# High and low parts of every stationary operand alternate in memory, 8 bytes apart

## The chip, the core and the metric

The kernel runs on one core of one Trainium2 chip. The metric is the device time of one execution in microseconds (us). Times are the median of repeated runs. A profiled execution gives the views that are read here: busy time of each engine, groups of instructions, waits, the chain of work that ended last, and timelines.

## The reference

The kernel computes a transformer block on `x` of 2048 rows and 640 columns, in float32. Cut to what matters:

```python
mod = (silu(c) @ w_mod).reshape(1, 6, 1, 640)        # sa, ca, ga, sb, cb, gb
h = layernorm(x) * (1 + ca) + sa
q, k, v = split_heads(h @ wqkv)                      # 32 heads of 20
pq, pk = q @ w_phi[head], k @ w_phi[head]
phi = concat([softmax(p), softmax(-p)])              # for q and for k
kv, z = phi_k.T @ v, phi_k.sum(rows)
o = (phi_q @ kv) / (phi_q @ z + 1e-6)
x = x + ga * (o @ wo)
h = layernorm(x) * (1 + cb) + sb
r = relu(h @ w1 + b1) ** 2                           # 640 -> 1728
out = x + gb * (r @ w2 + b2)                         # 1728 -> 640
```

## The kernel before, in words

TensorE multiplies a stationary operand (up to 128x128, put in place by a weight load) with a moving operand that streams through. All large products are made in float32r. To keep float32 accuracy, each operand is held as two parts: a high part (the value rounded to float32r) and a low part (what is left over). A product is then three matmuls that add up in PSUM: high by high, high by low, low by high. `three` writes that list and `mm` (the helper whose line is L81 in the profile) issues it. Since every matmul has its own weight load, the high part of a stationary operand is loaded twice and the low part once for each product.

ACT writes the high part (a copy that rounds), and VectorE (DVE) writes the low part (`lo`, the helper whose line is L91: the full value minus the high part). High and low parts of an operand lie in one tile, but in separate runs: 128 or 256 high values one behind the other, and the low values 1 to 2.5 KB further on. A weight load so reads 128 neighbouring values per partition, 512 bytes.

The rows are worked in 16 tiles of 128 rows, in pairs (`j`, 256 rows). There are four stages:

1. The set-up (0 to about 20 us): `fold` multiplies the projection weights with `w_phi`.
2. The projections (to about 250 us). For each pair, the normalised rows are turned (`t1`, `t_out`) into `HT[j]`, a tile made by `ht` with the axes chunk, part, row. `proj` multiplies it, as the stationary operand, with the folded weights `wk`, `wq` and with `wv` as the moving operand. Each projection tile has two halves: 15 matmuls with 384 moving columns (380 for v) and 15 with 256 (260 for v). In the profile these are `pk`, `pq` and `pv`.
3. The attention output (about 250 to 380 us). `num` makes the numerators in PSUM; `num_hi` and `num_lo` write their parts into `OT[j]`, again a tile of `ht`. For the first two pairs (`DIRECT`) the low part is not made by DVE: a matmul with minus the identity (`neg`, L975) subtracts the high part in PSUM, with the high part as its moving operand. `do_wo` multiplies `OT[j]`, stationary, with `wo`: `pwo`, again 384 and 256 columns.
4. The feed-forward part (about 380 us to the end). `up` has the weights `W1[f]` stationary (tiles `w`) and the turned rows `H2[j]` (tiles `h`, from `ht`) moving: 256 columns. Its output is squared, and for the later pairs recombined (`sums`) for a product scheme with fewer block products. `split_a` and `split_s` write the parts of the squared values and of their sums into tiles `ra` and `rs`. These are stationary in `prod`, with `w2` (tiles `w` and `ring`) moving: `acc` with 384 columns, `acc3x`, `accx` and some of `acc` with 256.

The order of the instructions on each engine is written out by hand in most of the kernel (`manual_schedule`), and a scheduler places the rest. `H2`, `wk`, `wq`, `wv`, `wo` and `w2` are moving operands; `HT`, `OT`, `W1`, `RA` and `RS` are stationary. The last block of `W1` (f = 13) has only 64 columns, and its high and low parts together fill one 128-column load; it is made by the same function.

Of the kernel before, what the change touches and what calls it, by code (L numbers as in the profile page):

```python
# [8 lines left out]
F32 = mybir.dt.float32  # L9
F32R = mybir.dt.float32r  # L10
# [5 lines left out]
P = 128  # L16
# [6 lines left out]
NC = D // P  # L23
# [31 lines left out]
def kernel(  # L55
# [23 lines left out]
    def mm(o, terms, first=True, last=True, skip=False):  # L79
        for i, (a, b) in enumerate(terms):  # L80
            nc.tensor.matmul(  # L81
                o, a, b,
                start=first and i == 0, stop=last and i == len(terms) - 1,
                skip_group_check=skip,
            )
# [4 lines left out]
    def lo(out_lo, full, hi, eng=None):  # L90
        (eng or nc.vector).tensor_tensor(out_lo, full, hi.bitcast(F32), op=ALU.subtract)  # L91
# [18 lines left out]
    def tok2(tag, name, at=0, pool=None):  # L110

        bufs = 1
        if tag == "w":
            tag = f"w{next(w_at)}"
        elif pool is None:
            bufs = BUFS.get(tag, 1)
        t = (pool or mem).tile([P, 2 * D + (W2_AT if tag == 'late' else 128 if tag in W_LONG else 0)], F32, tag=tag, name=name, bufs=bufs)
        return t[:, at : at + 2 * D].rearrange("p (s d) -> p s d", s=2)

    def row(tag, name):  # L120
        return (pc if tag in ("s3", "s4") else mem).tile([P, D], F32, tag=tag, name=name, bufs=BUFS[tag])
# [4 lines left out]
    def wslot(name, tag="w", pool=None):  # L126
        return tok2(tag, name, W2_AT if name.startswith("w2_") else 0, pool).bitcast(F32R)

    def ht(name, j, at=(32, 0)):

        t = mem.tile([P, NC * 512 + (32, 96)[j % 2]], F32R, tag=f"h{j % 2}", name=name, bufs=1)
        at = at[j % 2]
        return t[:, at : at + NC * 512].rearrange("p (d s n) -> p d s n", d=NC, s=2)

    def small(shape, tag, name, bufs=2):
        return (pc if tag in ("mx", "sk", "dn", "dd") else tiny).tile(shape, F32, tag=tag, name=name, bufs=bufs)
# [4 lines left out]
    def tp(name):  # L141
        return psA.tile([P, 512], F32, tag="tp", name=name)
# [152 lines left out]
    def mod_turn(part, p, *cs_):  # L295
        t = MT.setdefault(part, None) or row("s1", f"mt{part}")
        MT[part] = t
        a, n = cs_[0] * P, len(cs_) * P
        for i, c in enumerate(cs_):
            src = by_turn(MA[part])[:, c] if part in (3, 4) else MA[part][:, c * P : (c + 1) * P]  # L300
            nc.tensor.transpose(p[:, i * P : (i + 1) * P], src, ident)
        nc.scalar.activation(t[:, a : a + n], p[:, :n], AF.Copy)

    def mod_sum(part, dest):
        with tc.issue_after(newest(ET_.DVE)):
            nc.vector.tensor_reduce(dest, MT[part].rearrange("p (a b) -> p a b", b=P), axis=AX.X, op=ALU.add)
# [47 lines left out]
    def t_in(xn, d, p, mixed=False):  # L354
        for i in range(2):
            src = by_turn(xn[:, i])[:, d] if mixed else xn[:, i, d * P : (d + 1) * P]
            nc.tensor.transpose(p[:, i * P : (i + 1) * P], src, ident)  # L357
# [7 lines left out]
    def t_out(cols, hT, d, nm, p, hf=None):  # L365
        if hf is None:
            hf = row("s3", f"hf{nm}_{d}")[:, :256]
        nc.scalar.activation(hf, p[:, :256], AF.Identity, bias=cols[:, d : d + 1], scale=cols[:, 5 + d : 6 + d])
        nc.scalar.activation(hT[:, d, 0], hf, AF.Copy)  # L369
        lo(hT[:, d, 1], hf, hT[:, d, 0])  # L370


    HT, PK, EK, EQ, PQ = {}, {}, {}, {}, {}
# [3 lines left out]
    def newest(engine):  # L377
        return next(i for i in reversed(nc.cur_bb.bb.instructions) if i.engine == engine)
# [2 lines left out]

    def t1(j, *ds, more=None):
        if 0 in ds:
            HT[j] = ht(f"hT{j}", j)
        p = tp(f"ta{j}_{ds[0]}")
        for k, d in enumerate(ds):
            t_in(XB[j], d, p[:, 256 * k : 256 * k + 256])
        if more:
            mod_turn(more[0], p[:, 256:], 4)
        for k, d in enumerate(ds):  # L390
            t_out(cols_a, HT[j], d, f"a{j}", p[:, 256 * k : 256 * k + 256])
        DONE[:] = newest(ET_.Activation), newest(ET_.DVE)
        if more:
            mod_sum(*more)

    def proj(nm, t, *between, cut=CUT):
        p = pj(f"p{nm}{t}")
        j, i = divmod(t, 2)
        s = slice(i * P, (i + 1) * P)
        for h, (a, b) in enumerate(cut):  # L400
            terms = []
            for d in range(NC):
                w = W[nm, d]
                terms += three(HT[j][:, d, 0, s], HT[j][:, d, 1, s], w[:, 0, a:b], w[:, 1, a:b])
            done = 0
            for k, at, hook in between:
                if k == h:
                    mm(p[h][:, : b - a], terms[done:at], first=(done == 0), last=False)
                    hook()
                    done = at  # L410
            mm(p[h][:, : b - a], terms[done:], first=(done == 0))
        return p
# [183 lines left out]

    TR = [half(0, 0), half(1, 0), half(1, 1), half(2, 0), half(2, 1)]
    mem.tile([P, 48], F32, tag="gap", name="gap", bufs=1)
    HT[0], HT[1] = ht("hT0", 0), ht("hT1", 1)
    mem.tile([P, 80], F32, tag="gap2", name="gap2", bufs=1)  # L600
    PP = [pj(f"pk{t}") for t in range(0)]

# [101 lines left out]
    for t in range(2, NT - 2):  # L704
        j, i = divmod(t, 2)
# [4 lines left out]
        if t == NT - 4:  # L710
            t1(j + 1, 0, 1)
# [6 lines left out]
        p = proj("v", t, *([(1, 0, lambda: t1(j + 1, 4))] if t == NT - 3 else []), cut=V_CUT)  # L718
# [74 lines left out]
    def bank(nm):  # L793
        return psB.tile([P, 512], F32, tag="m", name=nm)
# [56 lines left out]
    ET, EU, EPT, OT = {}, {}, {}, {}  # L851
# [92 lines left out]
            nc.scalar.activation(t[:124], p[:124].rearrange("p (s n) -> p s n", s=2), AF.Copy)  # L944

    def num(j):
        OT[j] = ht(f"ot{j}", j)
        ps = [bank(f"numa{j}"), bank(f"numb{j}"), tp(f"numc{j}")]
        for g in range(5):
            for c in range(2):  # L950
                mm(ps[g // 2][64 * c : 64 * c + 64, (g % 2) * 256 : (g % 2) * 256 + 256],
                   [(kvd[:, g, 64 * c : 64 * c + 64], EPT[j, g][:124, c])], first=(g % 2 == 0), last=False, skip=True)
        NUM[j] = ps
# [57 lines left out]
    def prep_load(k, f, w):  # L1011
        n = FS[f]
        W = W1 if k == "1" else W2
        if k == "1":
            w = w.rearrange("p s (k n) -> p s k n", k=NC)
        W[f] = w
        i = preps.index((k, f))
        if EARLY_ROWS <= i < EARLY_ROWS + 4:
            if i % 2 == EARLY_ROWS % 2:
                RAWT.append(tok2(f"w{W_AT[(-19, -16)[len(RAWT)]]}", f"rawt{i}"))  # L1020
            raw = RAWT[-1][:, (i - EARLY_ROWS) % 2]
        else:
            raw = row("s1", f"rw{k}_{f}")
        if k == "1":
            raw = raw.rearrange("p (k n) -> p k n", k=NC)
        if k == "1":
            nc.sync.dma_start(raw, w1[f * P : (f + 1) * P].rearrange("p (k n) -> p k n", k=NC))
        else:
            for r in range(P // n):
                nc.sync.dma_start(raw[r * n : r * n + n], w2[f * P : f * P + n])  # L1030
        RAW[k, f] = raw
# [176 lines left out]
    for j in range(NB):  # L1208
        nxt = j + 1 < NB
        b, c = 2 * j + 5, 2 * j + 6  # L1210
# [53 lines left out]
        if nxt:  # L1264
            num(j + 1)
            num_hi(j + 1)
# [7 lines left out]
        if j == 7:  # L1274
            t2(0, 4)
            p = tp("gbt")[:NC, :P]
# [32 lines left out]
    p3 = ctx.enter_context(tc.tile_pool(name="p3", bufs=1, reuse_waits="tile"))  # L1309
# [4 lines left out]
    FT, RA, RS = {}, {}, {}  # L1314
# [31 lines left out]
    def plain(j, n):  # L1346
        return j < PLAIN or n == NF // 2 - 1 or j == NB - 1 and n >= NF // 2 - LAST
# [7 lines left out]
    def split_a(j, n, parts=(0, 1)):  # L1355
        t = FT[j, n]
        if 0 in parts:
            tag = "rs" if j < PLAIN and (NP * j + n) % 2 or (j, n) == (NB - 1, NP - 1) else "ra"
            RA[j, n] = p3.tile([P, 2, 4, P], F32, tag=tag, name=f"ra{j}_{n}").bitcast(F32R)
        a = RA[j, n]  # L1360
        if n < NP - 1:
            nc.scalar.activation(a[:, 0, :3], t[:, :3], AF.Copy)  # L1362
            lo(a[:, 1, :3], t[:, :3], a[:, 0, :3])
        elif 0 in parts:
            nc.scalar.activation(a[:, 0, 0], t[:, A11], AF.Copy)
            lo(a[:, 1, 0], t[:, A11], a[:, 0, 0])
        if plain(j, n) and 0 in parts:
            nc.scalar.activation(a[:, 0, 3], t[:, A21], AF.Copy)
            lo(a[:, 1, 3], t[:, A21], a[:, 0, 3])
        if n == NP - 1 and 1 in parts:  # L1370
            m = FS[-1]
            nc.scalar.activation(a[:m, 0, 1:3], t[:m, 1:3], AF.Copy)
            lo(a[m:, 0, 1:3], t[:m, 1:3], a[:m, 0, 1:3])

    def split_s(j, n):
        t = FT[j, n]
        a = RS[j, n] = p3.tile([P, 2, 4, P], F32, tag="rs", name=f"rs{j}_{n}").bitcast(F32R)
        nc.scalar.activation(a[:, 0], t[:, S1 : S4 + 1], AF.Copy)
        lo(a[:, 1], t[:, S1 : S4 + 1], a[:, 0])

# [408 lines left out]
```

## Time and profile before

| what | value |
|---|---|
| time, median of 3 runs | 747.2 us (746.77 to 747.63) |
| time of the profiled execution | 746.64 us |
| its span, first to last instruction | 744.9 us |
| PE busy | 738.1 us (99%), 6523 matmuls |
| weight loads (PEld) busy | 720.6 us (97%), 6523 loads |
| DVE busy | 598.8 us (80%) |
| ACT busy | 453.1 us (61%) |
| granted TensorE clock | 1.000 |

PE is the matmul side of TensorE, and PEld its weight loads, which overlap the matmul before. The recorded end of a matmul or a load is modelled and they are pipelined: a matmul recorded at 276 ns can be followed by the next one 113 ns later. What a matmul takes of the time is therefore read from the distance of starts: from a row of the chain or the timeline that merges many of them, its length is divided by their count. Differences between two recorded means of the same kind of matmul can be read directly.

### The profile page before, as it was taken

How to read it: one execution, taken by the hardware profiler on the slowest of the kernel's cores; microseconds unless marked ns; L12 is line 12 of the kernel's file. 1: busy time of each engine (PE TensorE's matmuls, PEld its weight loads, DVE VectorE, ACT ScalarE, POOL GpSimd, SP SyncE). 2: the span in 40 equal slices, each digit the busy share in tenths (PEclk: the TensorE clock that was granted, in tenths of full speed). 3: DMA queues.
4: the chain of work that ended last, by engine and by line, in shares of the span. 5: the costliest groups of instructions: out<-in, count | busy, mean ns of one | idle time of the engine just before them, and what ended most of it. 6: DMA issues, size and time to landing. Idle time of an engine off the chain costs nothing.

```text
span 744.9 us, 16612 instructions
## 1 busy us (share of the span) xinstructions
PE 738.1 (99%) x6523; PEld 720.6 (97%) x6523; DVE 598.8 (80%) x1089; ACT 453.1 (61%) x1028; POOL 169.1 (23%) x352
## 2 busy tenths in 40 slices
PE   9999999999999999999999999999999999999997
PEld 9999999999999988998999999999999999999997
DVE  6598988987999999999755777877786776777766
ACT  5767566657863355567687667475574747647431
POOL 2000101001100337547303040231321313222110
PEclk9999999999999999999999999999999999999999
DMA  8812341343331254754885567897667768667461
GB/s 330 339 37 106 111 134 59 107 143 107 126 124 72 83 184 152 173 137 106 209 251 166 154 199 255 271 312 211 180 190 201 214 184 240 187 176 213 129 183 36
DMA packets 58800, 126.46 MB, mean 170 GB/s; under 512 B 7438, under 2 KB 16403, under 8 KB 58723
## 3 DMA queue, kind: packets, MB, share of 16 engines
q1 hardware_dynamic: 38636, 79.20, 32.4%
q0 software_dynamic: 17504, 40.90, 22.1%
q10 hardware_dynamic: 2583, 5.30, 1.9%
q8 instruction: 51, 0.84, 0.5%
q14 instruction: 26, 0.21, 0.1%
HBM read 100.74 MB, written 29.89 MB: 175 GB/s over the span
## 4 chain that ended last, share of the span: by engine, by line
PE 88%; DVE 6%; ACT 3%; POOL 1%; issue 1%; ACTq 0%; DVEq 0%; POOLq 0%
PE up L81 25%; PE acc L81 18%; PE pk L81 8%; PE pwo L81 8%; PE pv L81 8%; PE pq L81 6%; PE acc3x L81 5%; PE te L943 2%; PE kvp L448 1%; DVE dn L875 1%; PE foldk L275 1%; PE numa L81 1%; PE ta L357 1%; DVE scr L873 1%; PE foldq L275 1%
## 5 line engine op out<-in xcount | busy, mean ns | idle before, releaser
L81 PE MATMUL up<-h,w 128*128 128x256 f32 x1640 | 204.6, 276 | 0.1
L81 PEld LDWEIGHTS up<-h,w 128*128 128x128 f32 x1640 | 196.5, 188 | 0.7 <-DVE h L91 0.5
L1338 ACT ACTIVATE ft<-up,b_t 128x256 f32<-128x256 f32 x104 | 49.2, 473 | 95.6 <-PE up L81 95.2
L81 PE MATMUL acc<-w,ra 128*128 128x384 f32 x452 | 97.5, 335 | 0.0
L1339 DVE TENSOR_TENSOR ft<-ft 128x256 f32<-128x256 f32 x104 | 43.8, 421 | 43.0 <-ACT ft L1338 41.5
L81 PE MATMUL pwo<-wo,ot 128*128 128x384 f32 (+1 forms) x480 | 78.1, 313 | 0.0
L81 PE MATMUL pq<-wq,hT 128*128 128x384 f32 (+1 forms) x480 | 75.8, 312 | 0.0
L81 PEld LDWEIGHTS acc<-w,ra 128*128 128x128 f32 x452 | 72.7, 188 | 0.8 <-DVE ra L91 0.6
L81 PE MATMUL pk<-wk,hT 128*128 128x384 f32 (+1 forms) x480 | 73.1, 309 | 0.0
L81 PE MATMUL pv<-wv,hT 128*128 128x380 f32 (+1 forms) x480 | 73.0, 309 | 0.0
L81 PEld LDWEIGHTS pwo<-wo,ot 128*128 128x128 f32 x480 | 69.5, 188 | 2.8 <-issue 2.7
L81 PEld LDWEIGHTS pq<-wq,hT 128*128 128x128 f32 x480 | 71.3, 188 | 0.7 <-issue 0.5
L81 PEld LDWEIGHTS pv<-wv,hT 128*128 128x128 f32 x480 | 71.3, 188 | 0.0
L81 PEld LDWEIGHTS pk<-wk,hT 128*128 128x128 f32 x480 | 70.8, 188 | 0.5 <-ACT hT L369 0.2
L91 DVE TENSOR_TENSOR ra<-ft,ra 128x384 fp32r<-128x384 f32 (+2 forms) x86 | 36.8, 448 | 32.6 <-ACT ra L1362 18.8
L1448 POOL DMA_DIRECT2D ring_a<-td_a x34 | 18.5, 543 | 117.2 <-PE acc L81 103.5
L1362 ACT ACTIVATE ra<-ft 128x384 fp32r<-128x384 f32 x48 | 25.2, 526 | 28.4 <-DVE ft L1339 22.3
L81 PE MATMUL acc3x<-w,ra 128*128 128x256 f32 x231 | 39.5, 278 | 0.0
L81 PEld LDWEIGHTS acc3x<-w,ra 128*128 128x128 f32 x231 | 37.2, 188 | 0.0
L439 DVE TENSOR_REDUCE sk<-ek 128x64 f32<-128x1280 f32 x16 | 23.7, 1482 | 15.1 <-ACT ek L434 10.7
L1353 DVE TENSOR_TENSOR ft<-ft 128x128 f32<-128x128 f32 x136 | 33.3, 286 | 1.2
L334 POOL TENSOR_SCALAR sma<-sma 128x2 f32<-128x2 f32 x6 | 3.1, 516 | 134.9 <-ACT xb L333 134.9
(255 smaller groups left out, 1442.5 us busy)
## 6 DMA issues: line engine op xcount, KB each, us to landing
ring_c<-td_c POOLq DMA_DIRECT2D x34, 384.0 KB, 4.0
ring_a<-td_a POOLq DMA_DIRECT2D x34, 384.0 KB, 3.4
ring_b<-td_b POOLq DMA_DIRECT2D x34, 256.0 KB, 3.6
esp<-eq SPq DMA_DIRECT2D x12, 640.0 KB
el<-esp SPq DMA_DIRECT2D x12, 640.0 KB
rw<-in_w SPq DMA_DIRECT2D x23, 320.0 KB
wm<-in_w_mod SPq DMA_DIRECT2D x20, 320.0 KB
xb<-in_x SPq DMA_DIRECT2D x8, 640.0 KB
```

The source lines that it names most:

```text
L81: nc.tensor.matmul(o, a, b, start=first and i == 0, stop=last and i == len(terms) - 1, skip_group_check=skip,)
L91: (eng or nc.vector).tensor_tensor(out_lo, full, hi.bitcast(F32), op=ALU.subtract)
L275: nc.tensor.matmul(p[g // 3][:, (g % 3) * 120 : (g % 3) * 120 + n], r, bd_t[:120, g * 120 : g * 120 + n], start=True, stop=True,)
L357: nc.tensor.transpose(p[:, i * P : (i + 1) * P], src, ident)
L439: nc.vector.tensor_reduce(s, heads(flat(e)), axis=AX.X, op=ALU.add)
L448: nc.tensor.matmul(kvp[0][32 * c : 32 * c + DH + 1, a - g % 3 * DH : a - g % 3 * DH + 2 * m].rearrange("p (s n) -> p s n", s=2)[:, :, h % ...
L943: nc.tensor.transpose(p[:124, a : a + P], EU[2 * j + i][:, 2 * g + c, :124], ident)
L1338: nc.scalar.activation(r, p, AF.Relu, bias=b1_t[:, f : f + 1])
L1339: nc.vector.tensor_tensor(r, r, r, op=ALU.mult)
L1353: nc.vector.tensor_tensor(t[:, o], t[:, a], t[:, b], op=op)
L1362: nc.scalar.activation(a[:, 0, :3], t[:, :3], AF.Copy)
L1448: nc.gpsimd.dma_start(RING[j, n, r], TD[n][r].bitcast(F32R))
```

## The change

Every stationary operand that has two parts changes its order in memory. The axes of its tile are now chunk, column, part, where they were chunk, part, column (or part, chunk, column): high and low values alternate, so neighbouring values of one part are 8 bytes apart, and the low value lies 4 bytes behind its high value. Sizes and places of the tiles stay the same. The edit is made by a new flag of `ht` and by views:

```diff
-    def ht(name, j, at=(32, 0)):
+    def ht(name, j, at=(32, 0), mixed=False):
...
-        return t[:, at : at + NC * 512].rearrange("p (d s n) -> p d s n", d=NC, s=2)
+        t = t[:, at : at + NC * 512]
+        return t.rearrange("p (d n s) -> p d s n", d=NC, s=2) if mixed else t.rearrange("p (d s n) -> p d s n", d=NC, s=2)
...
-            HT[j] = ht(f"hT{j}", j)
+            HT[j] = ht(f"hT{j}", j, mixed=True)
...
-    HT[0], HT[1] = ht("hT0", 0), ht("hT1", 1)
+    HT[0], HT[1] = ht("hT0", 0, mixed=True), ht("hT1", 1, mixed=True)
...
-        OT[j] = ht(f"ot{j}", j)
+        OT[j] = ht(f"ot{j}", j, mixed=True)
...
-            w = w.rearrange("p s (k n) -> p s k n", k=NC)
+            w = w.rearrange("p s d -> p (s d)").rearrange("p (k n s) -> p s k n", k=NC, s=2) if n == P else w.rearrange("p s (k n) -> p s k n", k=NC)
...
-            RA[j, n] = p3.tile([P, 2, 4, P], F32, tag=tag, name=f"ra{j}_{n}").bitcast(F32R)
+            RA[j, n] = p3.tile([P, 2, 4, P], F32, tag=tag, name=f"ra{j}_{n}").rearrange("p a b n -> p (a b n)").rearrange("p (b n s) -> p s b n", b=4, s=2).bitcast(F32R)
...
-        a = RS[j, n] = p3.tile([P, 2, 4, P], F32, tag="rs", name=f"rs{j}_{n}").bitcast(F32R)
+        a = RS[j, n] = p3.tile([P, 2, 4, P], F32, tag="rs", name=f"rs{j}_{n}").rearrange("p a b n -> p (a b n)").rearrange("p (b n s) -> p s b n", b=4, s=2).bitcast(F32R)
```

`H2` and the temporary rows that also come from `ht` keep the old order, and so does the 64-column block of `W1`. The order of the instructions on every engine, their count and what each waits for stay as they were; ACT's and DVE's writes of the parts, DVE's reads of the high part and TensorE's loads step by 8 bytes where they stepped by 4. The six matmuls with `neg` read the high part of `OT` as their moving operand, so these too step by 8 bytes. DMAs touch none of these tiles.

## The prediction

> **What bounds the kernel now.** I read the page first: how busy each engine is.
>
> ```profile
> PE 738.1 (99%) x6523; PEld 720.6 (97%) x6523; DVE 598.8 (80%) x1089; ACT 453.1 (61%) x1028; POOL 169.1 (23%) x352
> ```
>
> PE is busy for all but 7 us of the 744.9 us span, so waiting is not the matter. Next the busy times by stage: projections, attention output, and four stretches of the feed-forward part (columns: length, then PE, PEld, DVE, ACT, POOL, granted clock, DMA share, GB/s).
>
> ```profile
> 60.00:250.00 190.00, 188.98 (x2241) 185.87 (x2240) 170.47 (x218) 120.37 (x258) 17.86 (x27) 1.00 0.32 105
> 278.00:370.00 92.00, 91.41 (x688) 82.09 (x687) 83.28 (x101) 56.51 (x128) 54.00 (x97) 1.00 0.60 152
> 384.00:480.00 96.00, 96.00 (x755) 95.56 (x754) 71.06 (x157) 63.64 (x148) 17.56 (x48) 1.00 0.67 212
> 480.00:560.00 80.00, 80.00 (x631) 80.00 (x630) 61.49 (x157) 52.66 (x127) 22.34 (x43) 1.00 0.81 230
> ```
>
> From 384 us on PE never stands still, and in the two stages before it stands still for 1.6 us of 282. The granted clock is 1.00 throughout. The time is therefore the sum of the distances at which matmuls follow each other. This change touches nothing but how the stationary operands are laid out, so I need those distances. The chain of work gives them (start, length, count): each row is an unbroken run of matmuls.
>
> ```profile
> 81.02 4.40 PE pk L81 x30
> 125.91 4.43 PE pk L81 x30
> 139.90 4.30 PE pk L81 x30
> 732.06 2.83 PE up L81 x25
> 735.58 2.08 PE acc L81 x12
> ```
>
> A 256-column matmul takes 2.83/25 = 0.113 us, a 384-column one 2.08/12 = 0.173. The three `pk` rows are the same 30 matmuls (15 of each width) on three row tiles, and yet differ by up to 0.13 us. 15 x (0.173 + 0.113) is 4.29, the best of them. So there is a small loss of up to 3% that comes and goes with something that is not the work itself. The recorded means, by shape, show where it sits:
>
> ```profile
> L81 PE MATMUL up<-h,w 128*128 128x256 f32 x1640 | 204.6, 276 | 0.1
> L81 PE MATMUL acc<-w,ra 128*128 128x384 f32 x452 | 97.5, 335 | 0.0
> L81 PE MATMUL pwo<-wo,ot 128*128 128x384 f32 x240 | 47.3, 342 | 0.0
> L81 PE MATMUL pk<-wk,hT 128*128 128x384 f32 x240 | 46.7, 340 | 0.0
> L81 PE MATMUL pq<-wq,hT 128*128 128x384 f32 x240 | 46.1, 342 | 0.0
> L81 PE MATMUL pv<-wv,hT 128*128 128x380 f32 x240 | 44.3, 336 | 0.0
> L81 PE MATMUL acc3x<-w,ra 128*128 128x256 f32 x231 | 39.5, 278 | 0.0
> L81 PE MATMUL pwo<-wo,ot 128*128 128x256 f32 x240 | 32.9, 285 | 0.0
> L81 PE MATMUL pq<-wq,hT 128*128 128x256 f32 x240 | 32.3, 282 | 0.0
> L81 PE MATMUL pk<-wk,hT 128*128 128x256 f32 x240 | 31.6, 278 | 0.0
> L81 PE MATMUL acc<-ring_a,rs 128*128 128x384 f32 x102 | 23.1, 334 | 0.0
> L81 PE MATMUL acc<-w,rs 128*128 128x256 f32 x102 | 17.2, 277 | 0.0
> L81 PE MATMUL acc<-ring_b,rs 128*128 128x256 f32 x102 | 17.1, 276 | 0.0
> L81 PE MATMUL acc3x<-w,rs 128*128 128x256 f32 x102 | 17.1, 276 | 0.0
> ```
>
> The least means are 276 for 256 columns and 334 for 384. The feed-forward part is close to them; the projections and `pwo` lie 2 to 9 ns above.
>
> **The change part by part.** Order, count and waits of all instructions stay, so no instruction moves and no wait is added or removed. Five prices are left.
>
> First, the distance of matmuls in an undisturbed run. Does the load that runs beside a matmul slow the stream? The matmuls with `neg` answer, since two of them have no load beside them and two do (PE and PEld, start and length).
>
> ```profile
> 267.28 0.50 PE L975 MATMUL numb<-ot,neg 128*128 128x512 f32 x1
> 267.27 0.19 PEld L975 LDWEIGHTS numb<-ot,neg 128*128 128x128 f32 x1
> 267.55 0.19 PEld L975 LDWEIGHTS numc<-ot,neg 128*128 128x128 f32 x1
> 267.61 0.33 PE L975 MATMUL numc<-ot,neg 128*128 128x256 f32 x1
> 282.00 0.40 PE L975 MATMUL numb<-ot,neg 128*128 128x512 f32 x1
> 282.23 0.28 PE L975 MATMUL numc<-ot,neg 128*128 128x256 f32 x1
> 282.00 0.19 PEld L975 LDWEIGHTS numc<-ot,neg 128*128 128x128 f32 x1
> ```
>
> At 282.00 the next load starts with the matmul, and the next matmul follows after 0.23 us. At 267.28 the matmul first has to wait for its own load, and the next load comes only at the end: recorded 0.50 against 0.40, so 0.10 for the exposed load and again 0.23 for the stream. The stream runs at 0.44 to 0.45 ns a column with or without a load beside it. The change to the load's reading pattern can therefore not be expected to free the stream itself: price 0 for that, with the end below nothing in the second rival.
>
> Second, the losses above the least means. Over these: pk 6 x 240, pq and pwo 8 x 240 each, pv 2 x 240, acc 1 x 452 (384 or 380 columns: 6.2 us); pk 2, pq 6 and pwo 9 x 240, acc3x 2 x 231 (256 columns: 4.5 us); in all 10.7 us. Part of it is not the stream's: in `pq` and `pwo` other work is put between matmuls, and the first matmul after it carries a load that nothing hides, which the change leaves alone. The rest depends on how load and stream lie to each other, as the `pk` rows show: same addresses from tile to tile, other lengths. A contiguous load moves through 64 bytes while the stream moves through 128 (128 columns against 256 in the same 0.113 us), so they drift against each other. With a step of 8 bytes a load covers 1 KB in the time in which a 256-column stream covers 1 KB: they keep step. I take half of the 10.7 us as the gain, 5 us; ends 0 and 10.7.
>
> Third, the load itself. It must take less than 0.113 us or it becomes the bound of the 256-column matmuls. What a load needs when it reads one value behind the other, and when it steps, is shown by turning matmuls (128 columns, little to stream):
>
> ```profile
> 262.00 1.15 PE L943 MATMUL te<-ident,ezb 128*124 128x128 f32 x9
> 120.10 0.65 PE L301 MATMUL mc<-ident,wm 128*128 128x128 f32 x4
> 151.91 0.73 PE L301 MATMUL mc<-ident,wm 128*128 128x128 f32 x4
> ```
>
> Nine `te` in 1.15 us, less the last one's length of about 0.27, are 0.11 us each with loads of neighbouring values. Of the two `mc` rows the first loads neighbouring values and the second steps by 20 bytes (`by_turn`): 0.08 us more for four, 20 ns a load. So a step of 20 bytes costs up to 20 ns. For a step of 8 bytes the ends are 0 and 20 ns on top of 0.11 us; the first 3 ns are hidden under the 0.113. I take 0, being the end that is nearer to 8 bytes if the cost comes from reaching too few values in one piece of memory; the third rival takes the other way.
> [...]
>
> Fourth, the writes. DVE's `lo` now reads and writes with a step of 8 bytes, ACT writes with it. The only row with DVE reading at a step (20 bytes) is the transposing one:
>
> ```profile
> L1128 DVE STREAM_TRANSPOSE xm<-xx 128x640 f32<-128x640 f32 x16 | 21.8, 1362 | 2.7 <-ACT xx L1165 2.7
> L91 DVE TENSOR_TENSOR w<-rw,w 128x640 fp32r<-128x640 f32 x22 | 17.5, 826 | 2.8 <-ACT w L1037 2.5
> L91 DVE TENSOR_TENSOR ot<-numa,ot 128x512 fp32r<-128x512 f32 x6 | 4.1, 683 | 1.5 <-ACT ot L966 1.5
> ```
>
> 1362 against 826 for 640 elements is 1.65 times, and it is another operation: the far end. In the feed-forward part DVE has 18 of 80 us to spare, so even that stays beside the matmuls. In the attention stage it has 8.7 of 92 us; three `ot` operations a pair (two of 0.68, one of 0.41) at 1.65 times are 1.2 us for each of six pairs, 7 us, of which nearly all fits. I take 0; ends 0 and +5.
>
> Fifth, the six `neg` matmuls stream the high part with the new step: 4 x 0.23 + 2 x 0.12 = 1.2 us in all, taken at 0, doubled at worst: +1.2.
>
> The sum against the profiled execution: 746.6 - 5 = 741.6. Its span is 744.9 and 1.7 lie around it; the median of the runs shown is 0.6 above it, so 742.
>
> **The rivals.** Nothing changes: the loads are hidden before and after, and the lengths of the runs stay as mixed as they are. For it speaks the `neg` reading: a load beside a stream costs the stream nothing. Against it speak the unequal `pk` rows. It gives 747.
> [...]
>
> Freed further: if the stream's 0.113 us came from the two reading side by side after all, the 256-column matmuls could fall to the 0.11 of a load. These are 1560 of `up` (the 80 of its last block keep their layout), 231 + 720 of `acc3x`, `pk`, `pq`, `pwo` and 306 on `rs`: 2817, times 3 ns is 8.5 us, and with the whole 10.7 us 19: 728. The `neg` rows speak against it.
>
> Slower: the load becomes the bound. If a load with 8-byte steps takes 0.118 us, 8 ns more, 5 ns of that show in each of the 2817 matmuls: 14 us, 761. It decides from 3 ns on; the 384-column ones hide it with 60 ns to spare. For it: the load must touch twice as much memory, a step of 20 bytes costs up to 20 ns, and only 3 ns are free. Against it: 8 bytes is a much smaller step. At 4 ns more it is 1 ns a matmul, 750; at the far end of 20 ns it is 48 us.
>
> That the change doesn't do what it says is no rival: all five kinds of stationary operands take the new step.
>
> **How the numbers follow.** Forecast (in step) 0.34, freed further 0.10, nothing 0.22, load as bound 0.34. A run tells 0.2%, 1.5 us, from no change. Forecast and freed further are faster but for a few per cent; of nothing, most stays within 1.5 us, and its rest goes both ways, as the mixture of run lengths may shift by a us or two: faster 0.43, same 0.20, slower 0.37. Both signs hold much, so the forecast's own range stands here: 736 to 747, the ends of its gain. The whole range has to reach the freed case at 728 with 2 us for noise and order, and 762 for the load at 8 ns; beyond lie a dearer load and a freer stream, together 2 in 10.
>
> **What would show it.** Right: `up` rows stay at 276 or lower, the 384-column means of `pk`, `pq` and `pwo` come down to 334 to 336 and the 256-column ones to 276 to 278, and all `pk` runs of 30 take the same 4.3 us or less. The load as bound: all 256-column means rise by the same few ns, `up` included, while the 384-column ones stay. DVE at fault: the L91 rows of `ra`, `rs`, `ot`, `hT` grow, and PEld waits for them. Freed: `up` falls below 0.113 us a matmul. The prediction is wrong if the means of `up` or `acc` change by more than 2 ns, for it leaves the undisturbed stream as it is.

## The result, and the profile after

The changed kernel takes 765.5 us (median of 4 runs, 765.17 to 766.0) against 747.0 before: a ratio of 1.0247, interval 1.0229 to 1.0265. It is 18.5 us slower where 742 was forecast, and 3.5 us beyond the upper end of the range. Of the rivals, "the load becomes the bound", priced at 761, is nearest.

First the busy times of the page, and the first and the last of the four stretches by stage (columns as before: length, then PE, PEld, DVE, ACT, POOL, granted clock, DMA share, GB/s).

```profile
PE 759.3 (99%) x6523; PEld 743.1 (97%) x6523; DVE 601.1 (79%) x1089; ACT 458.7 (60%) x1028; POOL 167.0 (22%) x352
```

```profile
60.00:250.00 190.00, 190.00 (x2244) 187.96 (x2242) 170.69 (x217) 121.58 (x256) 15.28 (x27) 1.00 0.32 105
480.00:560.00 80.00, 80.00 (x601) 80.00 (x600) 58.42 (x149) 47.80 (x114) 21.67 (x41) 1.00 0.81 232
```

PE stands still no more than before and the clock is still 1.00, but fewer matmuls fit into the same stretch: 601 instead of 631 in the last one. So it is the distances again. The chain of work of the changed kernel (start, length, count):

```profile
141.97 4.46 PE pk L81 x30
157.84 4.47 PE pk L81 x30
747.52 1.80 PE up L81 x15
751.09 2.94 PE up L81 x25
754.75 2.12 PE acc L81 x12
```

Fifteen `up` take 1.80 us, 0.120 us each, where it was 0.113. The run of 25 holds its own control: its last ten belong to the block of `W1` that kept its order, and 2.94 - 1.80 leaves 0.114 us for each of these. A 384-column `acc` takes 2.12/12 = 0.177 instead of 0.173. The `pk` runs of 30 are now all alike, as the forecast said, but at 4.46 and not at 4.3: 15 x (0.120 + 0.177) is 4.46.

The recorded means by shape of the changed kernel show that all of these groups moved:

```profile
L81 PE MATMUL up<-h,w 128*128 128x256 f32 x1640 | 214.9, 282 | 0.1
L81 PE MATMUL acc<-w,ra 128*128 128x384 f32 x452 | 98.8, 339 | 0.0
L81 PE MATMUL pk<-wk,hT 128*128 128x384 f32 x240 | 47.2, 342 | 0.0
L81 PE MATMUL acc3x<-w,ra 128*128 128x256 f32 x231 | 40.5, 282 | 0.0
L81 PE MATMUL pwo<-wo,ot 128*128 128x256 f32 x240 | 34.2, 290 | 0.0
L81 PE MATMUL pk<-wk,hT 128*128 128x256 f32 x240 | 32.7, 282 | 0.0
L81 PE MATMUL acc<-ring_b,rs 128*128 128x256 f32 x102 | 17.8, 283 | 0.0
L449 PE MATMUL kvp<-ek,vt 128*21 128x40 f32 x1024 | 11.9, 203 | 0.0
```

Added up over all groups of this view (busy time and the idle time just before it, after less before): `up` 10.3 us, the other 256-column groups 6.5, those of 384 and 380 columns 4.1, `neg` 1.0, the rest -2.3. That is 19.6, and the span grew by 19.4, from 744.9 to 764.3. The rest is mostly `kvp`, with 1.1 us less of busy and 0.9 us less of idle time; why was not looked into. Its row before, and two rows of the loads before:

```profile
L448 PE MATMUL kvp<-ek,vt 128*21 128x40 f32 x1024 | 13.0, 203 | 0.9 <-issue 0.9
L81 PEld LDWEIGHTS up<-h,w 128*128 128x128 f32 x1640 | 196.5, 188 | 0.7 <-DVE h L91 0.5 <-ACT h L369 0.2
L943 PEld LDWEIGHTS te<-ident,ezb 128*124 128x124 f32 x160 | 18.0, 139 | 0.2
```

After, the load itself is recorded longer, 194 ns for 188, and DVE's operation on `ot`, which makes low parts, takes 687 ns for 683:

```profile
L81 PEld LDWEIGHTS up<-h,w 128*128 128x128 f32 x1640 | 206.8, 194 | 0.5 <-DVE h L91 0.3 <-ACT h L370 0.2
L91 DVE TENSOR_TENSOR ot<-numa,ot 128x512 fp32r<-128x512 f32 x6 | 4.1, 687 | 2.4 <-ACT ot L967 2.4
```

The `neg` matmuls, which now stream their moving operand at the 8-byte step, start 0.45 us apart instead of 0.23 where they have 512 columns (timeline, start and length):

```profile
284.04 0.63 PE L976 MATMUL numb<-ot,neg 128*128 128x512 f32 x1
284.49 0.41 PE L976 MATMUL numc<-ot,neg 128*128 128x256 f32 x1
```

### The profile page after: what moved, and what is told of

Read it like the earlier page. It is cut to its first block, busy times and chain, and to the rows that moved or that the text cites. A ratio compares the mean times of both kernels' runs of the same rounds, so it can differ in the third digit from the quotient of the medians.

```text
span 764.3 us, 16612 instructions
## 1 busy us (share of the span) xinstructions
PE 759.3 (99%) x6523; PEld 743.1 (97%) x6523; DVE 601.1 (79%) x1089; ACT 458.7 (60%) x1028; POOL 167.0 (22%) x352
## 4 chain that ended last, share of the span: by engine, by line
PE 97%; DVE 1%; ACT 1%; issue 0%; POOL 0%; ACTq 0%; POOLq 0%
PE up L81 26%; PE acc L81 18%; PE pq L81 9%; PE pk L81 9%; PE pv L81 9%; PE pwo L81 8%; PE acc3x L81 5%; PE te L944 2%; PE kvp L449 1%; PE foldk L276 1%; PE numa L81 1%; PE ta L358 1%; PE numb L81 1%; PE foldq L276 1%; PE warm L617 1%; PE mrow L578 0%
## 5 line engine op out<-in xcount | busy, mean ns | idle before, releaser
L81 PE MATMUL up<-h,w 128*128 128x256 f32 x1640 | 214.9, 282 | 0.1
L81 PEld LDWEIGHTS up<-h,w 128*128 128x128 f32 x1640 | 206.8, 194 | 0.5 <-DVE h L91 0.3
L81 PE MATMUL pwo<-wo,ot 128*128 128x384 f32 (+1 forms) x480 | 80.1, 317 | 0.0
L81 PEld LDWEIGHTS acc<-w,ra 128*128 128x128 f32 x452 | 75.2, 195 | 0.3 <-DVE ra L91 0.3
L81 PEld LDWEIGHTS pwo<-wo,ot 128*128 128x128 f32 x480 | 71.8, 196 | 3.2 <-issue 2.9
L81 PE MATMUL pk<-wk,hT 128*128 128x384 f32 (+1 forms) x480 | 74.7, 312 | 0.0
L81 PEld LDWEIGHTS pk<-wk,hT 128*128 128x128 f32 x480 | 72.4, 195 | 0.4 <-issue 0.2
L1449 POOL DMA_DIRECT2D ring_a<-td_a x34 | 18.5, 543 | 122.3 <-PE acc L81 111.6
L1363 ACT ACTIVATE ra<-ft 128x384 fp32r<-128x384 f32 x48 | 26.9, 559 | 27.4 <-DVE ft L1340 21.1
```

What stands on the lines that cost most here:

```text
L81: nc.tensor.matmul(o, a, b, start=first and i == 0, stop=last and i == len(terms) - 1, skip_group_check=skip,)
L1449: nc.gpsimd.dma_start(RING[j, n, r], TD[n][r].bitcast(F32R))
```

## The experiments

Two theories stood at the start. Either a load with an 8-byte step is slow by itself (the named rival), or it is slow only because it now reads, all the time, in the same 64-byte half of 128 bytes as the stream. By their addresses, load and stream of `up` and `acc` start in opposite halves in the kernel before; with the step of 8 bytes a load passes through both halves, at the stream's pace by the numbers (128 values on 1 KB in 0.120 us, 256 columns on 1 KB in 0.113).

**Halves: the load by itself.** Each matmul of `up` is cut in two of 128 columns with the same weights. The stream then lasts about 0.057 us (half of 0.113) and the load sets the distance. Both kernels got the same edit:

```diff
-        mm(p, terms, first=(k == 0 or alone), skip=True)
+        for i, (a, b) in enumerate(terms):
+            for h in range(2):
+                nc.tensor.matmul(p[:, P * h : P * h + P], a, b[:, P * h : P * h + P],
+                    start=(k == 0 or alone) and i == 0 and h == 0, stop=i == len(terms) - 1, skip_group_check=True)
```

> The layout of before, but each product of up is made as two matmuls of 128 columns, so that every load of up has only 128 columns of stream beside it and the load sets the distance. Nothing is left out. Both theories: 3280 matmuls of up at the distance of a contiguous load, 0.109 to 0.112 us, so about 747 + 175 = 922 us.

> The changed layout with the same halved matmuls of up. Slow load (a load with 8-byte steps takes 0.12 us by itself, whatever streams beside it): 0.119 to 0.121 us a matmul of up, about 9 to 10 ns over the halved kernel with the old layout, 30 us or more in up alone. Collision (load and stream disturb each other while both read): the stream runs for only half of the load's time, so about half the loss, 0.113 to 0.116 us, 3 to 5 ns over the old layout, 10 to 16 us in up.

They took 929.5 and 958.4 us. A row of the chain and two of the timeline with contiguous loads (start, length, count):

```profile
907.08 3.30 PE up L1333 x30
906.92 3.46 PE L1333 MATMUL up<-h,w 128*128 128x128 f32 x30
906.98 3.40 PE L1333 MATMUL up<-h,w 128*128 128x128 f32 x29
```

With the 8-byte step, three rows of the chain and two of the timeline:

```profile
929.98 3.54 PE up L1334 x30
935.35 3.48 PE up L1334 x30
940.65 5.77 PE up L1334 x50
935.18 3.64 PE L1334 MATMUL up<-h,w 128*128 128x128 f32 x30
935.24 3.58 PE L1334 MATMUL up<-h,w 128*128 128x128 f32 x29
```

A row of the chain is counted from the recorded end of the matmul before it, which is why it starts later than the timeline's row; its length holds as many distances as it has matmuls. The second matmul of a run follows the first after only 0.06 us (906.92 and 906.98, 935.18 and 935.24), so this first distance has to be taken out. A contiguous load then takes (3.30 - 0.06)/29 = 0.112 us. With the step it takes (3.48 - 0.06)/29 = 0.118 in one run and (3.54 - 0.06)/29 = 0.120 in the other, and the last twenty of the 50, which kept their order, are back at 0.112 to 0.114 (5.77 less 3.54 or 3.48, by 20). So the step costs the load 6 to 8 ns with half a stream beside it. As a difference that lies between what the two theories wanted; as a time it is close to the 0.119 to 0.121 of the slow load. It is more than the 0.113 that a full matmul took before, and it comes within 2 ns of the 0.120 that the full matmuls of the changed kernel take.

**Shifted starts: does a collision exist?** The moving operand of `up` is moved by 64 bytes, in both kernels, so that load and stream start in the same half:

```diff
-            H2[j] = ht(f"h2_{j}", j, (0, 96))
+            H2[j] = ht(f"h2_{j}", j, (16, 80))
```

> The layout of before, with the moving operand of up (the turned rows h2) put 64 bytes lower, so that it starts in the same half of 128 bytes as the stationary one; they start in opposite halves now. Slow load: 747 us, up stays at 0.113 us a matmul. Collision by halves of 128 bytes: up rises, to about 0.118 us, 8 us in all, 755.

> The changed layout with the same shift of h2 by 64 bytes. Slow load: 765.5 us, no change, up at 0.120. Collision: a load with 8-byte steps moves through memory as fast as a 256-column stream, so starting in the same half must collide more than starting in opposite halves; up rises by 5 ns or more, 8 us or more, 774 us or more; if the halves matter the other way round, up falls towards 0.113, 755.

The kernel before goes to 760.3 us (ratio 1.0163, 1.0145 to 1.0182) although its loads are contiguous; the changed one stays where it was, 766.7 against 765.5 (1.0247 of before, 1.0230 to 1.0264). The chain of the shifted kernel before:

```profile
741.47 1.78 PE up L81 x15
744.97 2.97 PE up L81 x25
```

That is 0.119 us a matmul: with load and stream starting in the same half, a matmul of `up` takes 6 ns more than 113, although its load is contiguous. It is not the new start of the stream alone: by the tiles' addresses `wk` starts at the same place within 128 bytes in the kernel before, opposite to its load, and its 256-column matmuls stand at 278 there. So there is a loss of the kind that the collision theory asks for, 6 ns a matmul, and the starts of before avoid it; that the two meet in a half is the author's reading of it. The total is more than the 755 that was expected: by the groups' rows `up` takes 9.6 us more, and `acc` and `acc3x`, none of whose operands moved, together 3.4 us.

For the changed kernel the collision theory had asked for 774 or more, or for 755, and neither came; the slow load's "no change" did. That its loads meet the stream in both halves wherever they start would fit this, but it is argued and not shown.

**One part at a time.** One kernel has the new order in `up`'s weights alone, the other everywhere but there:

```diff
-            w = w.rearrange("p s (k n) -> p s k n", k=NC)
+            w = w.rearrange("p s d -> p (s d)").rearrange("p (k n s) -> p s k n", k=NC, s=2) if n == P else w.rearrange("p s (k n) -> p s k n", k=NC)
```

> Of the change only the weights of up (W1) take the 8-byte step. Both theories of a loss in TensorE: the part of up, 1560 matmuls by 6.5 ns, 10 us, so 757 us; acc, pk, pq and pwo as before. If instead the writes of ACT and DVE held PE up, this part (weights written once, long ahead) would cost nothing: 747.

> The change without W1: turned rows, numerators, squared values and their sums take the 8-byte step. Loss in TensorE: the rest of the 18.5 us, 8 us, so 755 to 756 us, with up back at 276. Writes: the whole 18.5 us, 765.

They took 758.3 us (1.0136, 1.0116 to 1.0156) and 758.7 (1.0139, 1.0119 to 1.0158). Rows by shape of the first, then of the second kernel:

```profile
L81 PE MATMUL up<-h,w 128*128 128x256 f32 x1640 | 215.0, 282 | 0.1
L81 PE MATMUL pk<-wk,hT 128*128 128x256 f32 x240 | 31.5, 278 | 0.0
```

```profile
L81 PE MATMUL up<-h,w 128*128 128x256 f32 x1640 | 207.1, 278 | 0.1
L81 PE MATMUL pk<-wk,hT 128*128 128x256 f32 x240 | 32.7, 283 | 0.0
```

Each group slows where its own stationary operand has the step. Slow writes of ACT and DVE are ruled out for `up`: its weights are written once, long ahead, and still cost the 10 us that were expected. The second kernel is 3 us slower than expected: `up` is 2.5 us longer than before (207.1 for 204.6) with untouched weights, and why was not tried. This is not paid a second time once `up` has a step of its own, where it takes 214.9 with the whole change and 215.0 with its part alone. The two costs add up to 2.75% where the whole change costs 2.47%, which the intervals do not tell apart.

**Wider steps: what is it that a load counts?** The parts of `W1` stay apart or alternate, and its five blocks take turns, so that neighbouring values of one load lie 20 or 40 bytes apart (the first and the second line with +):

```diff
-            w = w.rearrange("p s (k n) -> p s k n", k=NC)
+            w = w.rearrange("p s (n k) -> p s k n", k=NC) if n == P else w.rearrange("p s (k n) -> p s k n", k=NC)
...
+            w = w.rearrange("p s d -> p (s d)").rearrange("p (n k s) -> p s k n", k=NC, s=2) if n == P else w.rearrange("p s (k n) -> p s k n", k=NC)
```

> The kernel before with only W1 laid out with a step of 20 bytes (five chunks side by side; high and low parts in separate halves). By pieces of 64 bytes that a load touches (8 contiguous, 16 at 8 bytes, 40 at 20 bytes), if each further piece costs the same 0.8 ns: 26 ns more, 0.139 us a matmul, 40 us, 787. [...]

> The same with a step of 40 bytes (five chunks and both parts side by side). By pieces of 64 bytes (80 touched): 58 ns more, 0.171 us, 90 us, 837. [...]

920.6 us (1.2302, 1.2273 to 1.2331) and 936.9 (1.2523, 1.2497 to 1.2549): far more than the 787 and 837 that a count of 64-byte pieces gave, and only 16 us apart where it had them 50 apart. The chain, 20 bytes first, then 40:

```profile
895.69 3.40 PE up L81 x15
905.93 4.53 PE up L81 x25
```

```profile
916.16 3.53 PE up L81 x15
```

3.40/15 = 0.227 us a load at 20 bytes, and 3.53/15 = 0.235 at 40: twice the span, nearly the same price. (The ten untouched ones in the run of 25 take (4.53 - 3.40)/10 = 0.113.) A price that hardly grows with the span is one for each value. So it looks as if at 20 and 40 bytes every value needs a read of its own, 0.227/128 = 1.77 ns each. Reads of that length would fit the stream too: 256 contiguous columns are 1 KB in 0.113 us, the time of 64 such reads, which makes 1,024/64 = 16 bytes for each. From these two numbers comes a new theory, an estimate: **a line rate**. A line is here a piece of 16 bytes, the size just worked out; TensorE would take one in 1.77 ns for the load and one for the stream, and what counts would be how many lines an operand touches. An 8-byte step puts 128 values on 64 lines, 0.113 us; the 5 to 7 ns that the load takes above this the theory put down to its start, which no run shows.

**12 bytes: a test of the line rate.** Three of the five blocks of `W1` take turns (12-byte step), and two take turns (8-byte step); high and low parts lie apart as before. ACT and DVE need two instructions for each part of a block instead of one.

```diff
+            if n == P:
+                F = w.rearrange("p s k n -> p s (k n)")
+                W1P[f] = [F[:, :, 0:384].rearrange("p s (n k) -> p s k n", k=3), F[:, :, 384:640].rearrange("p s (n k) -> p s k n", k=2)]
...
-                terms += three(W1[f][:, 0, d], W1[f][:, 1, d], H2[j][:, d, 0], H2[j][:, d, 1])
+                terms += three(w1of(f, 0, d), w1of(f, 1, d), H2[j][:, d, 0], H2[j][:, d, 1])
```

> The kernel before with another order in up's weights alone: of the five blocks of contraction the columns of the first three take turns (12-byte step, 936 of the 1,640 matmuls of `up`), those of the other two take turns (8-byte step, 624), high and low parts in blocks of their own as before; 80 matmuls keep contiguous loads. Line theory: 128 columns with a 12-byte step lie on 96 lines, 96 x 1.77 = 170 ns and the 4 to 7 ns that the 8-byte step showed over its 64 lines, so 174 to 177 ns a matmul, between the 120 of the 8-byte step and the 225 of 20 bytes; those with 8 bytes 120 ns although no part alternates; about 747 + 936 x 0.062 + 624 x 0.0065 = 809 us. Rival, that every column more than 8 bytes from the last one has a read of its own, as 20 and 40 bytes showed: 225 ns, 747 + 936 x 0.112 + 4 = 856 us. Second rival, that the cost of the change is that high and low parts lie together and not the step: the 624 with 8 bytes stay at 113 ns.

It took 809.1 us (one run; before beside it 749.8). The line rate had asked for 809, or 62 us more than before; the 59 measured are near it, and that the totals meet is in part chance. Two rows of the chain, and three of the timeline, in which the second run is seen whole, from its second matmul on, and in its last six:

```profile
785.77 2.29 PE up L81 x15
781.94 2.24 PE up L81 x15
781.78 2.40 PE L81 MATMUL up<-h,w 128*128 128x256 f32 x15
781.90 2.28 PE L81 MATMUL up<-h,w 128*128 128x256 f32 x14
783.30 0.88 PE L81 MATMUL up<-h,w 128*128 128x256 f32 x6
```

A run of 15 holds nine at 12 bytes and then six at 8. In the second run the six start at 783.30, 1.52 us behind the first of the nine: they take 2.24 - 1.52 = 0.72 us, 0.120 each. Of the nine the first distance is short again (0.12), and the other eight take (783.30 - 781.90)/8 = 0.175. With the same six, the nine of the first run take (2.29 - 0.72)/9 = 0.174 us. 96 lines at 1.77 ns are 0.170, and the theory had asked for 0.174 to 0.177; a read of its own for every value would have been 0.227, 856 us in all. The few ns above the lines are seen at 8 and at 12 bytes but not at 20, where 128 lines alone are 0.227 (the 1.77 was taken from there); what they are was not tried. Turned round, 0.174 us are 98 reads for 1,536 bytes, 15.7 bytes each, near the 16 of the estimate. And since the parts lie apart here and the six still take 0.120, it is the step that costs and not that the parts alternate.

**Quarters: the load with hardly a stream.** `up` in four matmuls of 64 columns, same edit as the halves, to see whether the 0.118 to 0.120 stay.

> The kernel before with every matmul of `up` in four matmuls of 64 columns, each with its own load of the same 128x128 weights (all contiguous): 6,560 loads, and almost no stream beside them (64 columns are 28 ns at the 113.3 ns that 256 columns took). Every theory expects the load alone to set the pitch, as in the run in halves, 109.9 ns a load; 4,920 loads more than before at 109.9 ns and 1,640 times (109.9 - 113.3) ns give about 747 + 4,920 x 0.1099 - 5.6 = 1,282 us. It is the reference for its twin with the parts alternating.

> The changed kernel, `up` in quarters as in its twin. Line theory (the array takes one 16-byte line per 1.77 ns; 128 columns with an 8-byte step lie on 64 lines, 113 ns, and some 4 ns of start): the pitch of the loads stays at the 117 ns that the halves showed, whatever streams beside them, 7 ns over the contiguous twin; 6,080 loads with the 8-byte step make it some 44 us longer than the twin, about 1,330 us with the 6 us that the rest of the change cost. Collision theory (the load is slow only because the stream reads in the same 64-byte halves): half as long a stream as in the halves, so half the loss or less: 113 ns or under, at most 22 us longer than the twin apart from the rest's 6, about 1,305 us.

1,893.8 and 1,904.4 us: both expectations failed by some 600 us, because the granted clock fell, in the mean to 0.664 and 0.668. A table of stretches of the contiguous kernel, then of the other (columns as above):

```profile
1747.98:1760.62 12.64, 12.64 (x62) 12.64 (x61) 0.01 (x1) 0.00 (x0) 0.53 (x1) 0.50 0.17 49
1764.13:1767.36 3.23, 3.23 (x31) 3.23 (x31) 0.00 (x0) 0.00 (x0) 0.47 (x1) 1.00 0.42 122
```

```profile
1759.34:1771.98 12.64, 12.64 (x61) 12.64 (x61) 0.04 (x1) 0.00 (x0) 0.53 (x1) 0.50 0.17 49
1652.80:1656.09 3.29, 3.29 (x29) 3.29 (x30) 1.23 (x1) 0.00 (x0) 0.54 (x1) 1.00 0.60 181
```

The totals say nothing on the question, but the stretches at a clock of 1.00 do. Of each of them two rows of the timeline (start, length, count), the second row being the last three matmuls of the first; the contiguous kernel, then the other:

```profile
1764.47 3.07 PE L1333 MATMUL up<-h,w 128*128 128x64 f32 x26
1767.03 0.50 PE L1333 MATMUL up<-h,w 128*128 128x64 f32 x3
```

```profile
1653.15 3.11 PE L1334 MATMUL up<-h,w 128*128 128x64 f32 x25
1655.74 0.52 PE L1334 MATMUL up<-h,w 128*128 128x64 f32 x3
```

From the first start to the start of the last three lie 2.56 us for 23 matmuls, 0.111 each, and 2.59 for 22, 0.118 each: 6 ns for the step, with a quarter of a stream beside the load. So about 0.118 belongs to the load alone. At a clock of 0.50 both kernels take the same time for 60 loads, as the chain shows (the contiguous one first):

```profile
1747.98 12.64 PE up L1333 x60
```

```profile
1759.34 12.64 PE up L1334 x60
```

0.211 us a load in both, where it was 0.111 and 0.118 at a clock of 1.00: at 0.50 the step costs nothing that shows.

**A hidden load in the same half.** Part of down's weights, which move in `acc` and `acc3x`, is put 64 bytes lower in the kernel before. All loads stay contiguous.

```diff
-        return tok2(tag, name, W2_AT if name.startswith("w2_") else 0, pool).bitcast(F32R)
+        return tok2(tag, name, W2_AT - 16 if name.startswith("w2_") else 0, pool).bitcast(F32R)
```

> The kernel before with part of down's weights, the moving operand of `acc`, 64 bytes further on, so that in 904 of its 1,210 matmuls (452 of 384 columns, 452 of 256) load and stream start in the same half of 128 bytes; in 204 of 384 columns and 102 of 256 they stay in opposite halves. All loads stay contiguous; that of a 384-column matmul (110 ns alone) is hidden under 170 ns of stream. Collision theory (a read of the load in the half that the stream is reading costs the stream time, hidden or not): the 384-column ones that were moved rise from 173.7 ns by 3 to 6 ns as the changed kernel's did by 3.6, the 256-column ones by 6 ns as those of `up` did in the other shift: 452 x 0.0045 + 452 x 0.006 = 4.7 us more, about 752 us; those that were not moved stay. Line theory without collisions (only the number of 16-byte lines of the load counts, and only when it is longer than the stream): nothing changes, 747 us, and the 3.6 ns of the changed kernel's 384-column matmuls come from the doubled lines.

753.4 us (752.26 to 754.54), ratio 1.0062, 1.0042 to 1.0082: 4.6 us where the collision theory had asked for 4.7. By groups the match is in part chance. Rows by shape:

```profile
L81 PE MATMUL acc<-w,ra 128*128 128x384 f32 x452 | 99.5, 339 | 0.0
L81 PE MATMUL acc<-ring_c,ra 128*128 128x384 f32 x102 | 23.5, 338 | 0.0
L81 PE MATMUL acc<-ring_a,rs 128*128 128x384 f32 x102 | 23.1, 334 | 0.0
L81 PE MATMUL acc<-ring_b,rs 128*128 128x256 f32 x102 | 18.2, 287 | 0.0
```

The moved 384-column group rises by 4 ns, to the 339 of the changed kernel, although its load (0.112 us in the halves) is much shorter than its distance of 0.173 us. But the place is not as simple as the theory had it. The largest moved 256-column group, `acc3x` on `ra`, stays at 278, where 6 ns had been asked for. Of the groups on `ring` tiles, which were not moved, one stays (334), one rises by 3 (from 335) and one by 11 ns (287 for 276). So the starts of a matmul's own two operands are not the whole condition, as the groups that slowed unmoved in the shifted kernel before show too.

## Why the prediction was wrong

The step that failed is the third price, the load itself: "For a step of 8 bytes the ends are 0 and 20 ns on top of 0.11 us ... I take 0." No row of before and no run shows that 0, which was the author's choice between the ends. It is 6 to 8 ns: the load takes 0.118 to 0.120 us by the halves and the quarters, against 0.112 when it is contiguous, so that only 1 to 2 of the 3 ns of slack are there. By these times the load sets the 0.120 of the 256-column matmuls, and these groups lost 16.8 us. At most 2 ns of each distance are left for the collision that the shifts showed; whether it has a part in them was not tried apart.

A second term of the sum failed with it: the gain of 5 us did not come, for no group of products has a lower mean than before. And two terms that were put at nothing were not nothing: the 384- and 380-column groups, whose loads of 0.118 to 0.120 us are well below their distance of 0.17, lost 4.1 us, and `neg` 1.0. With the -2.3 of the rest this is 5 + 16.8 + 4.1 + 1.0 - 2.3 = 24.6 us, where the profiled execution lies 24.4 above the sum's 741.6. That the 4.1 us are the collision is argued from the 4 ns of the same kind that the shift of down's weights cost; it was not shown in the changed kernel.

Point by point:

- **First price** (a load beside a stream costs the stream nothing): wrong as a rule. The `neg` rows show it for one pair of addresses. The shift of `h2` cost 6 ns a matmul with contiguous loads, and the shift of down's weights 4 ns under a hidden load: matmuls slow by 2 to 5% in these two runs when only the place of the moving operand changes.
- **Second price** (in step, -5 us): right only in that all `pk` runs became equal. They are equal at a worse length, 4.46 us, because the 256-column half of each now runs at the load's 0.120 us; of a gain from keeping step nothing is seen.
- **Third price**: the mechanism was named in the rival, with the right rows hit (2817 matmuls of 256 columns) and the right size: 8 ns for the load and 5 ns showing, 14 us. Measured, the 256-column groups lost 16.8 us, about 6 ns each. What the rival missed is the 384-column groups, which it left alone for their 60 ns to spare and which lost 4.1 us, and the 1.0 us of `neg`; these and the missing 3 us of the 256-column groups, less the rest, are the way from 761 to 765.5, to about 1 us. The chance of 0.34 was no lower than that of the forecast, and the range ended at the rival's price with no room for these.
- The bound for it, "a step of 20 bytes costs up to 20 ns", was wrong by far: 20 bytes cost 115 ns, 0.227 for 0.112. The `mc` and `te` rows that it came from are turning matmuls, and a load of `te` is recorded at 139 ns where those of the products stand at 188. They are of another kind; what makes them so was not tried. Nor is a step of 8 bytes free: two values to each 16 bytes take a load 0.118 to 0.120 us, four take 0.112.
- **Fourth price** (writes): right, 0 (the `ot` row). **Fifth** (`neg`): the far end of +1.2 and not 0; measured +1.0. At 0.45 us for 512 columns on 256 lines it is 1.76 ns a line, within the rounding the 1.77 of the estimate, so the profile after held this figure in plain sight.

For a version faster than both, the runs point nowhere: contiguous loads, with `up` and `acc` starting in opposite halves, are the best of everything that was tried, and that is the kernel before (747.0 us).

## What to carry to other kernels

Count the 16-byte lines that an operand touches, not its values: in these runs the stream (0.113 us for 64 lines, 0.45 for 256), and a load with a step (0.174 us for 96 lines, 0.227 for 128), take about 1.77 ns a line, the load with 4 to 7 ns more at steps of 8 and 12 bytes. Compare this with the stream beside the load: of 0.113 us the contiguous load left 1 to 2 ns to spare, so a step of two values (0.118 to 0.120) was already too much. A price for such a step has to come from the same kind of load; if the profile has none, the slack (taken as 3 ns of 113) is the number to weigh, and a rival that decides at so little deserves more than a third.

## What the runs showed of the hardware that was not expected

- A load's time against its step: 0.112 us at 4 bytes, 0.118 to 0.120 at 8, 0.174 to 0.175 at 12, 0.227 at 20, 0.235 at 40. From 8 to 20 bytes it goes with the number of 16-byte lines (64, 96 and 128, at 1.77 ns each 0.113, 0.170 and 0.227); at 4 something else sets 0.112 (32 lines would be 0.057), and the clock stretches suggest that it goes with the granted clock (0.211 at 0.50 for 0.111 at 1.00). Why 8 and 12 bytes cost 4 to 7 ns more than their lines, and 40 bytes 8 ns more than 20, stays open.
- Moving `h2` by 64 bytes, so that load and stream of `up` start in the same half of 128 bytes, costs 1.6% of this kernel (760.3 against 747.8 us) with nothing else changed. When a place costs time is only partly understood, as the rows of unmoved groups in both shifts show; a shift by another distance was not tried.
- The granted clock fell to 0.50 in long stretches of the quarter runs, though PE and PEld were busy all the time there (12.64 of 12.64 us): with 64 columns streamed behind each load of `up` the mean of a run is 0.664 and 0.668, with 128 (the halves) it is 0.998 and 0.999. What lowers it was not tried.
